# First-pass weight conversion: the low part's subtraction moved from VectorE to GpSimd

## The chip, the cores and the metric

The kernel runs on one core of a Trainium2 chip. The metric is the device time of one execution in microseconds; the kernel before takes 1091.99 us, the median of three runs (1090.27 to 1093.1).

## The reference

Linear attention over four batches, and two feed-forward blocks on its output:

```python
def phi(x):
    proj = np.einsum('bhsd,df->bhsf', x, w_phi)
    proj = proj - np.max(np.abs(proj), axis=-1, keepdims=True)
    return np.concatenate([np.exp(proj), np.exp(-proj)], axis=-1)
q_p, k_p = phi(q), phi(k)
kv = np.einsum('bhsf,bhsd->bhfd', k_p, v)
num = np.einsum('bhsf,bhfd->bhsd', q_p, kv)
den = np.einsum('bhsf,bhf->bhs', q_p, np.sum(k_p, axis=2))[..., None] + 1e-06
x = (num / den)              # 2304 tokens x 512 after a transpose
h = x @ w_in                 # 512 x 2048
x = np.maximum(0.01 * h, h) @ w_out          # 2048 x 512
g = x @ w_gate                               # 512 x 1536
out = (g / (1 + np.exp(-g)) * (x @ w_val)) @ w_out2   # 1536 x 512
```

The weights of the feed-forward blocks arrive as 64-bit floating point numbers.

## The kernel before, in words

The four batches of 576 tokens (b = 0 to 3) go through the kernel one after the other. The feed-forward blocks of batch b form one pass over all weights, and the attention of batch b + 1 is spread between the units of that pass. The attention of batch 0 stands alone at the start.

Every feed-forward product is split into three: a number is written as a high part that TensorE takes exactly (type float32r) and a low part, the rest. A product is then high x high, high x low and low x high. A unit (`u_l1`, `u_gate`, `u_val`, `u_out`, L645 to L694) makes one 128x576 result from 24 matmuls of 128x288.

There are 68 weight tiles of 128x512: 16 of kind "1" (w_in), 12 each of "g" and "v" (gate and value), 16 of "2" and 12 of "3" (the two output weights). In the first pass (b = 0) each of them goes through these steps:

- `w_load` (L493): SyncE's queue loads the 64-bit numbers into a `wi` buffer (five of them). `early` does the same for eight gate tiles during the attention of batch 0, with `gp` buffers.
- `w_to_f32` (L510): ScalarE (L519, L520, and L523 for kinds g, v and 3) and VectorE (L524, or L528 and L529, then L534) make a float32 tile in a `wr` buffer (four of them). Kinds 1, g and v are stored in DRAM as `kept`.
- `w_split` (L548) calls `to_wtile` (L543): ScalarE copies the float32 tile into the high part (L544), and a subtraction on VectorE makes the low part, float32 tile minus high part (L546, by the helper `sub`, which is recorded as L59). The result is a `wi` buffer for kinds 1, g and v and a `wo` buffer for kinds 2 and 3. The `wr` buffer is free after the subtraction.
- The `wo` tiles are stored in DRAM as `parts` by a DMA from GpSimd's queue (L565), for the later passes.

In the second pass (b = 1) the float32 tiles are read back and split again, and the split tiles are stored; later passes load most tiles already split. `to_wtile` is also called for the tiles of sums of weights (names ending in X and Y), in the second and later passes.

The order of the work: a list of the weights by the unit that needs them, each four units ahead (`slots`, L1007), drives `splits` (L1025), which keeps loads, conversions and splits a few weights ahead of one another. The program's planner then orders the instructions on each engine by its own model of their times. The order of the units on TensorE, of ScalarE's high parts and of some loads is pinned by tokens ("units", "weights", "loads").

GpSimd has little else: it fills the ones beside the attention's values (L122, into `pk` buffers) and issues the stores of L565. The fills wait until TensorE's matmul of L202 has released the buffer.

Of the kernel before, what the change touches and what calls it, by code (L numbers as in the profile page):

```python
# [7 lines left out]
F32 = mybir.dt.float32  # L8
# [5 lines left out]
ALU = mybir.AluOpType  # L14
# [27 lines left out]
def linear_attention_two_mlps(ctx: ExitStack, tc, qT, kT, vt, w_phi, w1, w2, wg, wv, w3, cst, out):  # L42
    nc = tc.nc
    act, dve, pe, pool = nc.scalar, nc.vector, nc.tensor, nc.gpsimd
# [9 lines left out]
    def T(shape, dt, tag, bufs, pool=sb):  # L54
        uid[0] += 1
        return pool.tile(shape, dt, tag=tag, name=f"{tag}_{uid[0]}", bufs=bufs)

    def sub(o, a, b):
        dve.tensor_tensor(out=o, in0=a, in1=b, op=ALU.subtract)  # L59
# [415 lines left out]
    def parts_tile(key):  # L475
        tag = ("wi", 5)
        if key[0] in "23":
            tag = ("vhl", 1) if key[1] == QB and key[2] % CH == CH - 1 else ("wo", 5)
        wtile[key] = t = T([P, 2, 512], F32R, *tag)
        return t  # L480
# [59 lines left out]
        kept[kind, f] = d = dram.tile([P, 512], F32, name=f"kept_{uid[0]}")  # L540
        nc.sync.dma_start(out=d, in_=t)

    def to_wtile(t, r):  # L543
        i = act.activation(t[:, 0], r, AF.Copy)  # L544
        tc.stamp_issue_order_token(i.ins, "weights")
        sub(t[:, 1], r, t[:, 0].bitcast(F32))  # L546

    def w_split(key):  # L548
        if key not in wf:
            return  # L550
        r = wf.pop(key)
        kind, b, f = key
        if len(kind) == 2:
            wtile[key] = pair = []
            for k in range(2):
                t = T([P, 2, 256], F32R, "kvh" if kind[1] == "X" else "kvl", 4)
                to_wtile(t, r[:, 256 * k : 256 * k + 256])
                pair.append(t)
            return
        t = parts_tile(key)  # L560
        to_wtile(t, r)
        if kind in "23":
            uid[0] += 1
            parts[kind, f] = d = dram.tile([P, 1024], F32, name=f"parts_{uid[0]}")
            pool.dma_start(out=d, in_=t.rearrange("p a n -> p (a n)").bitcast(F32))  # L565
        if b != 1:
            return
        unkept.append(((kind, f), t))
        if kind == "1":
            if f % 2 == 0:  # L570
                wf["even"] = r
                return
            even = wf.pop("even")
            mix(even, r)
            for name, x in (("1X", even), ("1Y", r)):
                t = T([P, 2, 512], F32R, "wi", 5)
                to_wtile(t, x)
                unkept.append(((name, f // 2), t))

    def mix(r0, r1):  # L580


        lo, hi = slice(0, 256), slice(256, 512)
        dve.tensor_tensor(out=r1[:, hi], in0=r1[:, lo], in1=r1[:, hi], op=ALU.add)
        sub(r1[:, lo], r0[:, lo], r1[:, lo])
        sub(r0[:, lo], r1[:, hi], r0[:, lo])
        sub(r0[:, hi], r0[:, hi], r0[:, lo])
# [437 lines left out]
    def splits(i):  # L1025
        for k in slots[i]:
            ahead(loaded, w_load, done[0] + 2)
            ahead(conv, w_to_f32, done[0] + 2)
            ahead(done, w_split, done[0] + 1)
            keep_all_but(2 if done[0] < len(order) and order[done[0]][1] < 2 else 0)  # L1030
            ahead(loaded, w_load, done[0] + depth())
# [119 lines left out]
```

## Time and profile before

| | |
|---|---|
| median of three runs | 1091.99 us |
| profiled execution | 1094.43 us, span 1092.6 us |
| mean granted TensorE clock | 0.997 |
| TensorE busy | 1062.8 us (97%) |
| VectorE busy | 808.8 us (74%) |
| ScalarE busy | 656.2 us (60%) |
| GpSimd busy | 21.8 us (2%) |

Times within the span are in microseconds from its start. The attention of batch 0 ends, and the first units begin, at about 67 us; the last tile of the first pass is split at about 351 us. In the rows PE is TensorE, PEld its weight loads, DVE VectorE, ACT ScalarE, POOL GpSimd, SP SyncE. The ends of matmuls are modelled, so overlapping matmuls can make TensorE look full while they are spaced out; their count in a stretch shows the spacing.

### The profile page before, as it was taken

The numbers are of one execution on the slowest core, as the hardware profiler recorded it, in microseconds if no ns is written. First come the engines' busy times: TensorE is split into PE (matmuls) and PEld (weight loads), VectorE is DVE, ScalarE is ACT, GpSimd is POOL, SyncE is SP. The second block draws the span as 40 slices with busy tenths as digits, with TensorE's granted clock in tenths as the row PEclk, the third lists the DMA queues.
The fourth block names the chain that finished last, engine by engine and source line by source line (L and its number), as shares of the span: only waits on it lengthen the run. The fifth ranks groups of instructions, "written<-read, shape, count | busy, mean of one in ns | idle before, by whom it ended". The sixth has DMA issues, their size and how long they took to land.

```text
span 1092.6 us, 20353 instructions
## 1 busy us (share of the span) xinstructions
PE 1062.8 (97%) x7560; PEld 1023.3 (94%) x7560; DVE 808.8 (74%) x1761; ACT 656.2 (60%) x1467; POOL 21.8 (2%) x56
## 2 busy tenths in 40 slices
PE   7889999999999999999999988999999999999998
PEld 6668999989899999999999988999999999999998
DVE  6897797888899888779676864857779742458473
ACT  7878886768777787546553575644542334426441
POOL 1000100000000000000000000000000000000000
PEclk9999999999999999999999998999999999999999
DMA  9736767555666887767454386346978768748652
GB/s 326 235 114 204 240 208 259 172 183 177 210 201 230 335 304 268 263 237 242 164 177 145 111 332 235 126 175 228 313 243 297 287 216 303 275 157 306 216 178 96
DMA packets 98771, 245.61 MB, mean 225 GB/s; under 512 B 19952, under 2 KB 28400, under 8 KB 98672
## 3 DMA queue, kind: packets, MB, share of 16 engines
q1 hardware_dynamic: 94640, 229.62, 60.6%
q0 software_dynamic: 4032, 14.68, 3.4%
q8 instruction: 60, 0.98, 0.4%
q14 instruction: 39, 0.32, 0.1%
HBM read 178.73 MB, written 65.54 MB: 224 GB/s over the span
## 4 chain that ended last, share of the span: by engine, by line
PE 80%; DMA 8%; ACT 6%; DVE 4%; issue 1%; SPq 1%; ACTq 0%; DVEq 0%
PE pm L615 55%; PE pa L741 8%; PE pm L741 4%; PE pa L202 4%; PE pa L393 3%; DMA wi<-in_w_dram 2%; DMA wi<-parts 2%; PE pa L161 2%; DMA wr<-kept 1%; ACT wr L519 1%; DMA sums<-wr 1%; DVE wr L534 1%; PE pm L301 1%; PE pa L346 1%; ACT wi L520 0%
## 5 line engine op out<-in xcount | busy, mean ns | idle before, releaser
L615 PE MATMUL pm<-xh,wi 128*128 128x288 f32 x1664 | 351.7, 298 | 2.4 <-DVE es L656 1.8
L615 PE MATMUL pm<-gp,wo 128*128 128x288 f32 x2256 | 337.5, 297 | 0.8 <-DVE acc L682 0.5
L615 PEld LDWEIGHTS pm<-gp,wo 128*128 128x128 f32 x2256 | 311.1, 188 | 5.2 <-issue 1.9
L615 PEld LDWEIGHTS pm<-xh,wi 128*128 128x128 f32 x1664 | 271.8, 188 | 6.8 <-DVE es L656 2.3
L615 PE MATMUL pm<-xl,wi 128*128 128x288 f32 x832 | 246.7, 297 | 0.0
L615 PEld LDWEIGHTS pm<-xl,wi 128*128 128x128 f32 x832 | 156.3, 188 | 1.4 <-issue 0.6
L682 DVE TENSOR_TENSOR acc<-pm,acc 128x288 f32<-128x288 f32 x160 | 70.5, 450 | 45.2 <-PE pm L615 43.1
L59 DVE TENSOR_TENSOR gp<-es,gp 128x576 fp32r<-128x576 f32 x94 | 70.5, 751 | 29.9 <-ACT gp L62 29.2
L62 ACT ACTIVATE gp<-es 128x576 fp32r<-128x576 f32 x94 | 64.3, 688 | 27.9 <-DVE es L663 22.8
L741 PE MATMUL pm<-xh,wi 128*128 128x288 f32 x304 | 71.6, 303 | 6.0 <-DMA wi<-parts 5.2
L59 DVE TENSOR_TENSOR wi<-wr,wi 128x512 fp32r<-128x512 f32 x96 | 64.8, 682 | 13.2 <-ACT wi L544 12.8
L544 ACT ACTIVATE wi<-wr 128x512 fp32r<-128x512 f32 x96 | 59.5, 633 | 13.1 <-PE pm L615 5.2
L741 PEld LDWEIGHTS pm<-xh,wi 128*128 128x128 f32 x304 | 53.2, 193 | 7.8 <-DVE fl L59 3.7
L59 DVE TENSOR_TENSOR fl<-ff,fh 128x512 fp32r<-128x512 f32 (+1 forms) x72 | 50.9, 712 | 11.0 <-ACT fh L62 10.8
L520 ACT ACTIVATE wi<-wi 128x512 int32<-128x512 uint32 x60 | 41.5, 692 | 23.1 <-DMA wi<-in_wv_dram 10.7
L519 ACT ACTIVATE wr<-wi 128x512 f32<-128x512 f32 x60 | 41.2, 690 | 16.4 <-DMA wi<-in_w_dram 8.6
L396 ACT ACTIVATE dn<-pa 64x288 f32<-64x288 f32 x64 | 26.0, 406 | 36.1 <-PE pa L393 35.2
L62 ACT ACTIVATE fh<-ff 128x512 fp32r<-128x512 f32 (+1 forms) x72 | 47.0, 664 | 0.8
L643 ACT ACTIVATE es<-pm 128x288 f32<-128x288 f32 x72 | 28.8, 418 | 29.7 <-PE pm L741 17.1
L741 PE MATMUL pm<-xl,wi 128*128 128x288 f32 x152 | 45.6, 300 | 0.0
L534 DVE TENSOR_TENSOR wr<-wr,wi 128x512 uint16<-128x512 uint16 x60 | 44.9, 751 | 0.8
L202 PE MATMUL pa<-ff,pk 128*128 128x256 f32 (+1 forms) x160 | 42.6, 383 | 2.4 <-issue 1.9
(192 smaller groups left out, 2073.4 us busy)
## 6 DMA issues: line engine op xcount, KB each, us to landing
wi<-parts SPq DMA_DIRECT2D x96, 512.0 KB, 5.9
wo<-parts SPq DMA_DIRECT2D x77, 512.0 KB, 6.6
parts<-wi SPq DMA_DIRECT2D x56, 512.0 KB, 4.6
wi<-in_w_dram SPq DMA_DIRECT2D x44, 512.0 KB, 5.1
wr<-kept SPq DMA_DIRECT2D x72, 256.0 KB, 4.2
parts<-wo POOLq DMA_DIRECT2D x28, 512.0 KB, 5.1
kept<-wr SPq DMA_DIRECT2D x40, 256.0 KB, 4.2
wi<-in_wv_dram SPq DMA_DIRECT2D x12, 512.0 KB, 4.1
```

The source lines that it names most:

```text
L59: dve.tensor_tensor(out=o, in0=a, in1=b, op=ALU.subtract)
L62: act.activation(o, a, AF.Copy)
L202: pe.matmul(ps[:, 256 * h : 256 * h + 256], v[:n, h].rearrange("p a d -> p (a d)"), part[b, j, s][:n, h].rearrange("p a f -> p (a f)"), st ...
L393: pe.matmul(ps, w, x, start=(i == 0), stop=(i == len(ops) - 1))
L519: act.activation(t, high.bitcast(F32), AF.Abs, scale=REBIAS)
L520: act.activation(low, low.bitcast(U32), AF.Copy, scale=2.0**-29)
L534: dve.tensor_tensor(out=t16, in0=t16, in1=e16, op=ALU.add)
L544: i = act.activation(t[:, 0], r, AF.Copy)
L615: m = pe.matmul(ps, w, x[:, c], start=(i == 0), stop=(i == n - 1))
L643: act.activation(o, i, AF.Prelu, alpha=0.01)
L682: dve.tensor_tensor(out=acc[o][:, t], in0=ps, in1=acc[o][:, t], op=ALU.add)
L741: m = pe.matmul(ps, a, b, start=start and n == 0, stop=stop and n == 5, skip_group_check=True)
```

## The change

`to_wtile` gets an argument for the engine that subtracts. For the 68 tiles of the first pass `w_split` passes GpSimd, for all others VectorE as before. The operation, its operands and their sizes stay. Other callers of `to_wtile` are not touched.

```diff
-    def to_wtile(t, r):
+    def to_wtile(t, r, eng=dve):
         i = act.activation(t[:, 0], r, AF.Copy)
         tc.stamp_issue_order_token(i.ins, "weights")
-        sub(t[:, 1], r, t[:, 0].bitcast(F32))
+        eng.tensor_tensor(out=t[:, 1], in0=r, in1=t[:, 0].bitcast(F32), op=ALU.subtract)
...
         t = parts_tile(key)
-        to_wtile(t, r)
+        to_wtile(t, r, dve if b else pool)
```

## Rows read from the trace of the kernel before

**Rows 1.** The page's first part: busy time, share, instructions of each engine.
```profile
PE 1062.8 (97%) x7560; PEld 1023.3 (94%) x7560; DVE 808.8 (74%) x1761; ACT 656.2 (60%) x1467; POOL 21.8 (2%) x56
```

**Rows 2.** Busy time by stretch, all engines; stretch, length, engines, clock, DMA.
```profile
core 0: us, PE busy (x) PEld busy (x) DVE busy (x) ACT busy (x) POOL busy (x), PEclk, DMA share, GB/s
67.00:100.00 33.00, 30.90 (x170) 26.69 (x169) 25.04 (x65) 24.74 (x69) 1.97 (x5) 1.00 0.42 130
...
175.00:205.00 30.00, 29.54 (x217) 28.36 (x216) 23.97 (x46) 19.55 (x39) 2.12 (x4) 1.00 0.63 207
205.00:285.00 80.00, 78.25 (x550) 74.16 (x549) 69.08 (x148) 61.06 (x126) 2.66 (x5) 1.00 0.51 163
285.00:310.00 25.00, 23.95 (x162) 21.71 (x161) 23.12 (x47) 22.77 (x47) 1.59 (x3) 1.00 0.78 262
310.00:352.00 42.00, 42.00 (x303) 40.57 (x302) 38.56 (x84) 31.45 (x67) 2.13 (x4) 1.00 0.58 193
...
205.00:352.00 147.00, 144.20 (x1010) 136.45 (x1009) 130.76 (x277) 115.29 (x238) 6.38 (x12) 1.00 0.58 188
```

**Rows 3.** Waits of TensorE, 67 to 352 us: total, times, longest.
```profile
PE pm L615 <- DVE es L656: 1.7, 1, 1.7
...
PE pm L615 <- DVE wi L59: 0.2, 1, 0.2
```

**Rows 4.** The chain of waits, 0 to 360 us: start, duration, link.
```profile
74.53 0.69 DVE wi L59
...
185.48 0.69 DVE wo L59
...
194.40 0.68 DVE wo L59
...
299.64 0.70 DVE wi L59
300.36 1.30 ACT wr L519 x2
```

**Rows 5.** Timeline of VectorE around 195 us: start, duration, instruction, wait before.
```profile
193.78 1.29 DVE L59 TENSOR_TENSOR wo<-wr,wo 128x512 fp32r<-128x512 f32 x2 [2.65 <-ACT wo L544]
...
195.23 0.43 DVE L528 TENSOR_SCALAR wr<-wr 128x512 int32<-128x512 int32 x1
```

**Rows 6.** Groups of VectorE by line, 0 to 352 us.
```profile
L59 DVE TENSOR_TENSOR wi<-wr,wi 128x512 fp32r<-128x512 f32 x42 | 28.7, 685 | 5.6 <-ACT wi L544 5.3
```

**Rows 7.** Waits of ScalarE, 67 to 352 us: total, times, longest.
```profile
ACT wr L519 <- DVE wi L59: 2.8, 6, 1.0
```

**Rows 8.** Groups of GpSimd by line, whole span.
```profile
L565 POOL DMA_DIRECT2D parts<-wo x28 | 15.2, 544 | 250.3 <-DVE wo L59 240.9 <-DVE top L348 8.8
L122 POOL MEMSET pk<- 128x256 f32 x16 | 4.9, 315 | 28.7 <-PE pa L202 26.5 <-issue 1.9 <-POOLq L1135 0.3
L122 POOL MEMSET pk<- 128x128 f32 x8 | 1.6, 204 | 50.7 <-issue 25.1 <-PE pa L202 16.9 <-DMA cst_sb<-in_cst_dram 8.7
```

**Rows 9.** Waits of GpSimd, whole span: total, times, longest.
```profile
POOL pk L122 <- PE pa L202: 43.4, 13, 7.9
```

**Rows 10.** Timeline of GpSimd around 139 us: start, duration, instruction, wait before.
```profile
139.30 0.20 POOL L122 MEMSET pk<- 128x128 f32 x1 [7.44 <-PE pa L202]
```

**Rows 11.** Groups of VectorE by line, 205 to 352 us.
```profile
L534 DVE TENSOR_TENSOR wr<-wr,wi 128x512 uint16<-128x512 uint16 x27 | 20.2, 753 | 0.0
L524 DVE SCALAR_TENSOR_TENSOR wr<-wr,wi 128x512 int32<-128x512 int32 x27 | 18.4, 681 | 7.3 <-ACT wi L523 7.3
L59 DVE TENSOR_TENSOR wi<-wr,wi 128x512 fp32r<-128x512 f32 x25 | 17.0, 683 | 0.8 <-ACT wi L544 0.7
...
L59 DVE TENSOR_TENSOR gp<-es,gp 128x576 fp32r<-128x576 f32 x13 | 9.7, 748 | 2.6 <-ACT gp L62 2.5
L59 DVE TENSOR_TENSOR wo<-wr,wo 128x512 fp32r<-128x512 f32 x12 | 8.2, 682 | 0.2 <-ACT wo L544 0.2
```

## The prediction

> **What bounds the kernel now.** I began with the busy shares: TensorE is busy for 97% of the span, VectorE 74%, ScalarE 60%, GpSimd 2% [rows 1]. The change touches only the first pass over the weights (b = 0), so I then cut that pass into stretches [rows 2]. The granted clock is 1.00 in all of them, so no term here belongs to the clock. VectorE is the fullest engine beside TensorE: 130.76 of 147 us between 205 and 352 us, which is 89%.
>
> A busy TensorE can still run thinly, because the ends of its matmuls are modelled, so I counted. Between 310 and 352 us it is busy throughout and runs 303 matmuls, 138.6 ns each. At that rate the 550 of 205 to 285 us need 76.2 us of 80, the 162 of 285 to 310 us need 22.5 us of 25, and the 217 of 175 to 205 us need all 30. The mix is richer in slower attention matmuls at 67 to 100 us, and there I take the plain gap, 33.0 - 30.9 = 2.1 us [rows 2]. So what a perfectly fed TensorE could win back in 67 to 352 us is 3.8 + 2.5 + 2.1 = 8.4 us, an estimate. This is the ceiling of the gain. The loss has no such ceiling.
>
> Who causes those gaps? TensorE waits for a converted weight's low part by name for only 0.2 us; its longest wait on VectorE is 1.7 us for an evicted gate [rows 3]. The chain of waits names the subtraction more often: six pieces after 67 us among its longest ones are this subtraction on VectorE, about 0.7 us each [rows 4] (the first, the last and two between stand there). At 193.78 us two subtractions run back to back for 1.29 us and the first step of the next weight's conversion (L528) starts behind them at 195.23 us [rows 5]: there the chain runs through VectorE's order, not through the data.
>
> **The change, part by part.** *Removed from VectorE:* 40 subtractions into wi and 28 into wo; the row of 0 to 352 us has 42 for wi, the last two of them from the second pass [rows 6]. 68 x 0.684 = 46.5 us leave VectorE. Nearly all of it lies beside TensorE's work, so it counts for the end only where the chain holds it. Of the six pieces, five are followed by other VectorE work that doesn't read their result. The first two of these stand side by side (wi, then wo at 75.6 us) and would follow one another on GpSimd's queue just so; I count one of the two. Without these four the chain is shorter by 4 x 0.68 = 2.7 us. The sixth, at 299.64 us, is followed by a ScalarE conversion step (L519) [rows 4], which fits a wait for a `wr` buffer: such waits are 2.8 us in six cases [rows 7]. There the subtraction itself is what counts, and it gets slower.
>
> *Added to GpSimd:* 68 subtractions of 128x512. The trace shows none on GpSimd. Its nearest rows are fills: 315 ns for 256 columns and 204 ns for 128 [rows 8], which is 0.867 ns a column and 93 ns fixed. A subtraction passes three streams (two read, one written). If all overlap it costs 93 + 444 = 0.54 us; if none does, 93 + 3 x 444 = 1.42 us. I take 1.2 us, nearer the upper end, since this engine's fills are already slow with one stream. The load is 68 x 1.2 = 82 us in a queue that holds 21.8 us of work now [rows 1], so GpSimd has room.
>
> The Trainium skill (GPSIMD Engine Reference, section 3.1) gives 4497 ns for a tensor_tensor of 2048 fp32 columns; a quarter, as an estimate, is 1.12 us, and the sum would be the same.
>
> *Latency:* a low part is ready 1.2 us after ScalarE's high part plus GpSimd's own queue, against 0.68 us plus VectorE's queue. The queue of an 89% busy engine costs about one instruction, so this comes out even to 0.6 us later. The cover is the plan: a weight is asked for four units ahead, and a unit of 24 matmuls lasts 24 x 138.6 ns = 3.3 us, so some 13 us. It is thin only where the conversion chain itself is late. The six `wr` waits grow by up to 0.74 us each (1.42 - 0.68), 4.4 us on ScalarE, of which I count 1.5 us on the path.
>
> *Order on GpSimd's queue:* behind a subtraction stand the store of the same tile (28 of 0.53 us, now on the engine that made the data) and the fills of the value tiles. Fills wait for TensorE to release a buffer, 43.4 us in 13 cases, the longest 7.9 us [rows 9]; a subtraction queued behind one waits too. The last fill of these is at 139.3 us [rows 10], and until there 13 us of lead cover 7.9 us, so I cost them at nothing; without the cover one is worth at most 7.9 us. SyncE's loads into `wr` begin only with the second pass; the last subtractions of the first release those buffers, late by the latency above. The planner reorders the queues by its model; no row prices that, and I let it move the result by one or two of the gaps above (2 to 4 us), either way.
>
> *VectorE held by GpSimd's reads:* whether two engines can read SBUF at the same time is not shown by any row here, since the fills read nothing. If they can't, hold per subtraction lies between 0 and 1.42 us. In 205 to 352 us, 23 + 12 = 35 subtractions move [rows 11, 2]: VectorE falls from 130.8 to 130.8 - 35 x 0.683 = 106.9 us. The forms that read two tiles from SBUF and stay (L534, L524, gp's low part: 20.2 + 18.4 + 9.7 = 48.3 us) are 45% of that [rows 11], with small forms left out. A hold of 0.45 to 0.6 x 1.2 us, so 0.54 to 0.72 us, would hand back 19 to 25 us of the 23.9 us.
>
> The Trainium skill (SBUF — State Buffer, section "Who interferes with whom") speaks against this change: a VectorE instruction with two SBUF inputs contends with a GpSimd instruction that reads SBUF, and the one that comes second is blocked for the whole of the first. By that rule VectorE is no freer than before; no run here shows it yet.
>
> Sum for the likeliest case: the profiled execution took 1094.43 us (span 1092.6). -2.7 + 1.5 = -1.2 us gives 1093.2 us. That execution is 2.4 us above the median of the runs, 1091.99 us, so against the median it is 1090.8, rounded to **1091 us**. Its own range is 1088.7 to 1095.3.
>
> **Rivals.**
> - *Faster, because VectorE is really freed.* Without a hold VectorE drops to 106.9 of 147 us, and the gaps at 205 to 310 us close: -6.3 us, 1085.7 us; with the gap at 67 to 100 us, 1083.6 us. For it: in the chain the next conversion steps stand behind subtractions [rows 5]. Against it: VectorE also waits for ScalarE in this stretch (7.3 us for L523 alone [rows 11]), and ScalarE keeps all its work.
> - *Slower, because the pair takes turns.* If GpSimd's reading holds VectorE for the whole subtraction, 205 to 352 us decides: VectorE's room is 147 - 106.9 = 40.1 us over 35 subtractions, so the turn comes at 1.15 us of hold each. At 1.42 us the stretch needs 106.9 + 49.7 = 156.6 us, 9.6 us more than it has: 1101.6 us. At 1.2 us it is full, and any late eviction stops TensorE; then I expect +5 us, 1097 us. For it: conversions come in bursts, so the next weight's two-input steps want to run just then. Against it: VectorE spends half its time in forms that read one SBUF tile or PSUM.
> - *The change moves the work, but nothing changes,* since TensorE never waits for it: 1092 us. It lies inside the forecast's range and speaks for it: 0.2 us of named waits [rows 3].
>
> **How the numbers follow.** About 0.3%, 3.3 us, is what a measurement of this kernel can tell from no change. Forecast (with the rival that nothing changes): 0.40. Freed VectorE: 0.28, all of it faster by over 0.3%. Held VectorE: 0.32, slower by over 0.3%; the `wr` waits growing on the path are counted in it. The range goes from 1084.5, near the closed gaps, to 1101.5, the full hold at the upper price.
>
> **What would show it.** Right: 68 subtractions on GpSimd of 1.1 to 1.4 us; VectorE's busy time of 205 to 352 us within 8 us of before although 35 instructions are gone, its two-input forms longer on average (L534 above 0.75 us); TensorE's matmul count of that stretch as before. The freed case would show L534 and L524 unchanged at 0.75 and 0.68 us and over 560 matmuls in 205 to 285 us. The held case would show VectorE above 140 us of 147 there and TensorE waiting for evictions by VectorE or ScalarE. Wrong in the working itself: a subtraction on GpSimd above 1.42 us, waits for `wo` or `wi` low parts named on TensorE, or a difference that arises after 352 us.

## The result, and the profile after

The changed kernel takes 1104.76 us (median of six runs, 1099.19 to 1106.67) where the kernel before took 1092.09 us beside it: the ratio is 1.0108, with an interval of 1.0091 to 1.0126. It is slower by 1.1%, outside the stated range and on the side to which the prediction gave 0.32. Of the runs below, one execution, the profiled one of the fills beside the kernel before (1116.81 us), was in a slower state; its time is left out, and only lengths and places are read from its profile.

The page's first part of the changed kernel, answering [rows 1]:

```profile
PE 1066.3 (97%) x7560; PEld 1025.0 (93%) x7560; DVE 795.9 (72%) x1693; ACT 655.0 (59%) x1467; POOL 115.3 (10%) x124
```

The work moved as planned: 68 instructions fewer on VectorE, 68 more on GpSimd. But VectorE is only 12.9 us freer, not 46.5 us. The instructions that stayed on it are longer by 26 us in all. The rest of the 33.6 us is overlap: neighbouring instructions overlap in the trace (before the change VectorE's lengths add up to 905 us where it is busy for 808.8 us), so an instruction that goes frees less than its length.

Busy time by stretch of the changed kernel (columns as in [rows 2]):

```profile
67.00:100.00 33.00, 30.87 (x167) 26.50 (x167) 22.80 (x59) 24.55 (x67) 7.15 (x7) 1.00 0.43 135
100.00:205.00 105.00, 99.76 (x669) 95.25 (x668) 74.42 (x131) 76.20 (x180) 41.16 (x44) 0.97 0.66 223
205.00:352.00 147.00, 142.65 (x989) 133.78 (x988) 121.86 (x238) 114.04 (x232) 54.08 (x46) 1.00 0.57 191
```

The middle stretch in the kernel before, in the same view:

```profile
100.00:205.00 105.00, 104.54 (x728) 100.74 (x728) 85.98 (x171) 84.41 (x197) 8.75 (x19) 1.00 0.73 246
```

The count of matmuls tells where the time went. Between 100 and 205 us TensorE runs 669 instead of 728; at the 138.6 ns that the prediction took for one, 59 of them are 8.2 us. Between 205 and 352 us 989 instead of 1010 are 2.9 us [rows 2]. The sum, 11.1 us, is the whole difference of the spans (1102.4 - 1092.6 = 9.8 us) and a little more; the changed kernel was four matmuls ahead at 100 us. And VectorE is *less* busy in both stretches: it fell from 85.98 to 74.42 us and from 130.76 to 121.86 us [rows 2]. TensorE lost its time while VectorE had more room than before.

GpSimd's groups in the changed kernel (line, operation, count, busy us, mean ns, idle before):

```profile
L546 POOL TENSOR_TENSOR wi<-wr,wi 128x512 fp32r<-128x512 f32 x40 | 54.9, 1375 | 181.8 <-ACT wi L544 173.1 <-DMA kept<-wr 4.2 <-DMA pk<-in_vt_dram 2.2
L546 POOL TENSOR_TENSOR wo<-wr,wo 128x512 fp32r<-128x512 f32 x28 | 39.0, 1407 | 13.9 <-ACT wo L544 13.9
```

VectorE's groups of the changed kernel, 0 to 365 us:

```profile
L534 DVE TENSOR_TENSOR wr<-wr,wi 128x512 uint16<-128x512 uint16 x60 | 51.0, 851 | 1.2
L59 DVE TENSOR_TENSOR gp<-es,gp 128x576 fp32r<-128x576 f32 x29 | 25.9, 895 | 8.1 <-ACT gp L62 8.0
L529 DVE SCALAR_TENSOR_TENSOR wr<-wi,wr 128x512 int32<-128x512 int32 x32 | 24.9, 777 | 0.5
L524 DVE SCALAR_TENSOR_TENSOR wr<-wr,wi 128x512 int32<-128x512 int32 x28 | 22.3, 796 | 11.6 <-issue 6.9 <-ACT wi L523 4.6
L528 DVE TENSOR_SCALAR wr<-wr 128x512 int32<-128x512 int32 x32 | 16.3, 509 | 24.5 <-ACT wr L519 24.5
L411 DVE TENSOR_TENSOR xf<-pa,rb 64x288 f32<-64x288 f32 x32 | 14.3, 448 | 0.8
L663 DVE SCALAR_TENSOR_TENSOR es<-pm,es 128x288 f32<-128x288 f32 x24 | 10.6, 445 | 0.1
```

The same groups in the kernel before, in the same stretch (L524 took 681 ns there too [rows 11]):

```profile
L534 DVE TENSOR_TENSOR wr<-wr,wi 128x512 uint16<-128x512 uint16 x60 | 44.9, 751 | 0.8
...
L529 DVE SCALAR_TENSOR_TENSOR wr<-wi,wr 128x512 int32<-128x512 int32 x32 | 21.8, 684 | 0.6
L59 DVE TENSOR_TENSOR gp<-es,gp 128x576 fp32r<-128x576 f32 x29 | 21.7, 750 | 4.5 <-ACT gp L62 4.4
...
L411 DVE TENSOR_TENSOR xf<-pa,rb 64x288 f32<-64x288 f32 x32 | 14.3, 446 | 0.6
...
L528 DVE TENSOR_SCALAR wr<-wr 128x512 int32<-128x512 int32 x32 | 13.4, 423 | 11.4 <-ACT wr L519 11.4
L663 DVE SCALAR_TENSOR_TENSOR es<-pm,es 128x288 f32<-128x288 f32 x24 | 10.6, 445 | 0.2 <-PE pm L615 0.2
```

The forms with two inputs in SBUF grew on average: L534 from 751 to 851 ns, L529 from 684 to 777, gp's low part from 750 to 895, L524 from 681 to 796. So did the one-input L528, from 423 to 509 ns. The forms with one input in PSUM (L411, L663) kept their length to 2 ns. The Trainium skill (SBUF — State Buffer, section "Who interferes with whom") draws just this line: a VectorE instruction with two SBUF inputs contends with a GpSimd instruction that reads SBUF, one in a two-port mode with any GpSimd instruction, and one that has a single SBUF input and no such mode with none. The trace agrees on every form shown here, though it doesn't show which mode L528 runs in.

How a stretched conversion step stops TensorE is to be seen in the timeline of the changed kernel around its second stop (start, duration, engine, instruction, idle time before it and what ended it):

```profile
167.25 2.77 POOL L546 TENSOR_TENSOR wo<-wr,wo 128x512 fp32r<-128x512 f32 x2
167.58 1.30 DVE L528 TENSOR_SCALAR wr<-wr 128x512 int32<-128x512 int32 x1 [1.63 <-ACT wr L519]
...
168.91 1.67 DVE L529 SCALAR_TENSOR_TENSOR wr<-wi,wr 128x512 int32<-128x512 int32 x1
...
170.61 0.75 DVE L534 TENSOR_TENSOR wr<-wr,wi 128x512 uint16<-128x512 uint16 x1
...
171.43 0.33 SPq L505 DMA_DIRECT2D wi<-in_w_dram  x1
...
177.48 0.66 ACT L519 ACTIVATE wr<-wi 128x512 f32<-128x512 f32 x1 [3.38 <-DMA wi<-in_w_dram]
...
178.61 0.69 ACT L643 ACTIVATE es<-pm 128x288 f32<-128x288 f32 x2
```

and TensorE's first matmul behind them:

```profile
179.05 0.61 PE L615 MATMUL pm<-xh,wi 128*128 128x288 f32 x1 [2.58 <-ACT es L643]
```

Two subtractions run on GpSimd from 167.25 us for 2.77 us. VectorE's L528 and L529 start beside them and take 1.30 and 1.67 us instead of 0.42 and 0.68, so they end 1.87 us late. L534 behind them is the last reader of a `wi` buffer; only when it ends does SyncE issue the load of the next weight, at 171.43 us. ScalarE's next instruction is L519 of that weight, so ScalarE stands still for 3.38 us, and the eviction L643 stands behind it. TensorE waits 2.58 us for that eviction. If everything behind L529 had come 1.87 us earlier, some 0.7 us of that wait would be left, an estimate. In all, SyncE's loads of weights wait longer for L534 than before (0 to 360 us; before, then after):

```profile
SPq L505 <- DVE wr L534: 67.7, 20, 11.2
```

```profile
SPq L505 <- DVE wr L534: 84.3, 20, 9.6
```

The two longest groups of TensorE's waits, 67 to 352 us, in the changed kernel (total, times, longest):

```profile
PE pm L615 <- ACT es L643: 2.8, 2, 2.6
PE pm L615 <- ACT gp L62: 2.1, 1, 2.1
```

They are waits for ScalarE, whose own work the change leaves alone (0.2 and 0.3 us before). The other groups, up to 1.8 us each, name ScalarE and VectorE; none names GpSimd. The stops cost more than they last, as the stretches of 10 us with them show:

```profile
140.00:150.00 10.00, 7.89 (x44) 7.30 (x44) 6.03 (x12) 8.51 (x22) 2.71 (x3) 0.83 0.93 318
...
170.00:180.00 10.00, 7.42 (x47) 6.91 (x46) 4.24 (x8) 4.69 (x11) 1.60 (x4) 0.94 0.89 324
180.00:190.00 10.00, 10.00 (x67) 9.84 (x67) 7.37 (x13) 8.66 (x20) 2.60 (x2) 0.88 0.81 261
```

After each stop the granted clock falls, to 0.83, 0.94 and 0.88 on average, that is to the lower of its levels (1.2 instead of 2.4 GHz) for part of the stretch (the last two belong to the same stop). Over 100 to 205 us it is 0.97 instead of 1.00: some 3 of the 8.2 us, an estimate (0.03 x 105 us).

### The profile page after: what moved, and what is told of

Its sections match the earlier page's. It is cut to its first block, busy times and chain, and to the rows that moved or that the text cites. A ratio compares the mean times of both kernels' runs of the same rounds, so it can differ in the third digit from the quotient of the medians.

```text
span 1102.4 us, 20385 instructions
## 1 busy us (share of the span) xinstructions
PE 1066.3 (97%) x7560; PEld 1025.0 (93%) x7560; DVE 795.9 (72%) x1693; ACT 655.0 (59%) x1467; POOL 115.3 (10%) x124
## 4 chain that ended last, share of the span: by engine, by line
PE 64%; DMA 11%; ACT 8%; DVE 7%; issue 6%; POOL 2%; SPq 1%; POOLq 0%; DVEq 0%; ACTq 0%
PE pm L615 43%; PE pa L741 8%; DMA wi<-in_w_dram 5%; PE pm L741 4%; PE pa L202 2%; PE pa L393 2%; DMA wi<-parts 2%; DMA wi<-in_wv_dram 2%; POOL wi L546 1%; DVE wr L534 1%; DMA wr<-kept 1%; ACT wr L519 1%; PE pa L161 1%; DVE wr L529 1%; ACT wi L520 1%
## 5 line engine op out<-in xcount | busy, mean ns | idle before, releaser
L59 DVE TENSOR_TENSOR gp<-es,gp 128x576 fp32r<-128x576 f32 x94 | 74.7, 796 | 35.5 <-ACT gp L62 34.8
L546 POOL TENSOR_TENSOR wi<-wr,wi 128x512 fp32r<-128x512 f32 x40 | 54.9, 1375 | 181.8 <-ACT wi L544 173.1
L519 ACT ACTIVATE wr<-wi 128x512 f32<-128x512 f32 x60 | 41.0, 684 | 27.0 <-DMA wi<-in_w_dram 11.7
L534 DVE TENSOR_TENSOR wr<-wr,wi 128x512 uint16<-128x512 uint16 x60 | 51.0, 851 | 1.2
L643 ACT ACTIVATE es<-pm 128x288 f32<-128x288 f32 x72 | 29.9, 430 | 26.7 <-PE pm L741 16.0
```

The costliest lines, as they stand in the source:

```text
L519: act.activation(t, high.bitcast(F32), AF.Abs, scale=REBIAS)
L534: dve.tensor_tensor(out=t16, in0=t16, in1=e16, op=ALU.add)
L546: eng.tensor_tensor(out=t[:, 1], in0=r, in1=t[:, 0].bitcast(F32), op=ALU.subtract)
L643: act.activation(o, i, AF.Prelu, alpha=0.01)
```

## The experiments

Three theories were put against each other. **Hold:** GpSimd's reads of SBUF block VectorE's two-input and two-port forms; conversions, loads, ScalarE and TensorE follow as above. **Late low part:** the subtraction takes twice as long on GpSimd, whatever VectorE does. **Order:** the planner orders all engines anew (on ScalarE some 380 places differ between the orders of the two traces), and the new order happens to be worse. All ratios are to runs of the kernel before on the same chip (its medians there were 1093.1 to 1093.8 us).

**Fills in place of subtractions.** The low parts of the first pass are left out. The first fill also covers the high part's last column, so that it waits for the high part as the subtraction did.

```diff
-        eng.tensor_tensor(out=t[:, 1], in0=r, in1=t[:, 0].bitcast(F32), op=ALU.subtract)
+        flat = t.rearrange("p a n -> p (a n)").bitcast(F32)
+        # on GpSimd: three fills, from the high part's last column on
+        for n in (513, 513, 128): pool.memset(flat[:, 511:511 + n], 0.0)
```

> In place of each of the 68 subtractions GpSimd fills the low part with zeros by three fills of 513, 513 and 128 columns (about 1.3 us together, from the fills' 0.867 ns a column and 93 ns), which wait for the high part and read nothing; the low parts of the first pass are left out of the products. Theory hold (GpSimd's reads of SBUF block VectorE's two-input and two-port forms, the conversions come late, the loads behind them come late, ScalarE stands on a load and TensorE on ScalarE): the loss of 12.7 us is gone, 1084 to 1094 us, L534 back at 0.75 us and L529 at 0.68 us on average. Theory late low part (1.3 us on GpSimd instead of 0.68 us on VectorE, whatever VectorE does): 1099 to 1106 us. Theory order (the planner's other order alone): 1099 to 1106 us, since the work on each engine is planned as in the changed kernel.

Measured: 1098.56 us, ratio 1.0038 (1.0019 to 1.0058). Two thirds of the loss are gone with the reads. VectorE's groups in this kernel:

```profile
L534 DVE TENSOR_TENSOR wr<-wr,wi 128x512 uint16<-128x512 uint16 x60 | 45.3, 755 | 1.0
...
L529 DVE SCALAR_TENSOR_TENSOR wr<-wi,wr 128x512 int32<-128x512 int32 x32 | 22.0, 687 | 0.6
...
L528 DVE TENSOR_SCALAR wr<-wr 128x512 int32<-128x512 int32 x32 | 19.2, 600 | 26.9 <-ACT wr L519 26.7
```

L534 and L529 are back at their old lengths. The one-input L528 is even longer, 600 ns on average, so a writing GpSimd still blocks that one. The median L528 takes 427 ns as before; a few take up to 2.4 us. The longest starts while GpSimd makes fills without a gap and ends only behind the last of them:

```profile
163.53 2.69 POOL L546 MEMSET wo<- 128x513 f32 x7
164.08 2.42 DVE L528 TENSOR_SCALAR wr<-wr 128x512 int32<-128x512 int32 x1 [1.46 <-ACT wr L519]
```

Hold had predicted at most 1094 us and the others at least 1099. The time lies between, just below the others' bound, while the two-input forms did what hold had said. So the reads account for about two thirds of the loss, and 0.4% is left for blocked L528, lateness and order together.

**A shadow subtraction beside the kernel before.** VectorE does all its old work; GpSimd reads the same tiles for nothing.

```diff
         sub(t[:, 1], r, t[:, 0].bitcast(F32))
+        if shadow:      # b == 0
+            pool.tensor_tensor(out=scratch, in0=t[:, 0], in1=t[:, 0], op=ALU.subtract)
```

> The kernel before, VectorE subtracts as before; beside each first-pass tile GpSimd subtracts the high part from itself into a scratch tile that nobody reads: 68 reads of SBUF on GpSimd, and nothing waits for them but their buffers. Theory hold: VectorE is blocked and not relieved, at least as slow as the changed kernel, 1102 to 1125 us, VectorE's L534 above 0.82 us on average. Theory late low part: 1089 to 1095 us, for every low part is made by VectorE. Theory order: within 4 us of 1092 us.

Measured: 1112.86 us, ratio 1.0169 (1.0149 to 1.019), as hold said and against the other two: no wait in the trace names these results. L534 grew less than hold said (786 ns, not over 820), because here the subtractions take the blow, as they start together with their shadows. VectorE keeps its subtractions here and becomes nearly full: it is busy for 141.33 of the 147 us from 205 to 352 us, where TensorE runs 934 matmuls instead of 1010. So this run shows that the reads cost time. It does not tell a full VectorE from single late steps.

**The same with fills.**

> As the shadow subtraction beside the kernel before, but GpSimd only fills the same scratch tile three times (512, 512, 128 columns, about 1.3 us): it writes SBUF and reads nothing. Theory hold: 1089 to 1095 us, VectorE's forms at their old lengths. Theory late low part: 1089 to 1095 us. Theory order: this one has its own order, so any time within 4 us of the shadow subtraction's is what it predicts.

Measured: 1101.51 us, ratio 1.0062 (1.0044 to 1.008). All three theories missed: hold and late low part had said 1095 us at most, order within 4 us of 1112.86 us. It is not the control it was meant to be. The fills wait for nothing but their buffers, so GpSimd makes nearly all of them at the start, where it is busy for 66.15 of the first 67 us, and the last 15 from 94 to 99 us. L534 and L529 kept their lengths. L528 is at 596 ns on average because one of them took 5.21 us beside those last 15 fills; its median is 427 ns. A cast of 128x10, 0.16 us in the kernel before, started beside 87 fills in a row and ended with the last of them:

```profile
44.15 31.00 POOL L547 MEMSET shadow<- 128x512 f32 x87
```

```profile
59.13 16.05 DVE L316 CAST mm<-mq 128x10 fp32r<-128x10 f32 x1
```

So where GpSimd's instructions follow one another without a gap, the block of a one-input form can last as long as the row, not only as long as one instruction.

**More buffers for the float32 tiles.** The changed kernel, kinds 2 and 3 converted into four more buffers.

```diff
-        t = T([P, 512], F32, "wr", 4)
+        t = T([P, 512], F32, *(("kvl", 4) if key[0] in "23" else ("wr", 4)))
```

> The changed kernel with four more buffers for the float32 tiles: those of kinds 2 and 3 go into kvl buffers, which are idle in the first pass. Theory late low part, in the form that the float32 buffers are held longer by GpSimd and ScalarE waits for them (6.3 us of named waits in the changed kernel): at most 1099 us. Theory hold: 1101 to 1108 us, the waits for buffers shrink but VectorE's stretched forms stay.

Measured: 1120.64 us, ratio 1.0234 (1.0209 to 1.0258): both theories missed. The experiment did not remove what it was meant to remove: ScalarE waits 7.7 us for GpSimd's subtractions between 67 and 352 us, against 6.3 us in the change. So it says nothing on what the held `wr` buffers cost, and why it got slower still stays open.

**The shadow with 32 and with 256 columns.** The cleanest test: the same 68 instructions at the same places of the program, only the length of the read differs. (The planner's order on ScalarE still differs between these three traces, by some 200 to 330 places.)

> The shadow subtraction beside the kernel before, cut from 512 to 32 columns: the same 68 instructions at the same places, each reading SBUF for a sixteenth. Theory hold: the loss of the full shadow (1.7%) nearly goes, 1090 to 1098 us, VectorE's subtractions back at 0.68 to 0.72 us from 0.91 (wi) and 1.13 us (wo). Theory order: the 68 instructions upset the planner as before, 1104 to 1116 us.

> The shadow subtraction beside the kernel before with 256 columns: between 32 columns (ratio 1.0004) and 512 (1.0169). Theory hold, with a blocked time that grows with the columns read: GpSimd's instruction near 0.95 us, VectorE's subtractions into wo between 0.72 and 1.1 us, 1096 to 1106 us. Theory order: no dependence on the columns.

Measured: 1094.26 us, ratio 1.0004 (0.9987 to 1.0021) with 32 columns, and 1097.37 us, 1.0044 (1.0027 to 1.0062) with 256, against 1.0169 with 512. The loss grows with the columns that GpSimd reads, and with 32 columns none is measured. Order predicted no dependence. VectorE's subtraction into wo at 32, 256 and 512 columns:

```profile
L59 DVE TENSOR_TENSOR wo<-wr,wo 128x512 fp32r<-128x512 f32 x28 | 19.2, 700 | 0.2
```

```profile
L59 DVE TENSOR_TENSOR wo<-wr,wo 128x512 fp32r<-128x512 f32 x28 | 24.1, 872 | 0.2 <-ACT wo L544 0.2
```

```profile
L59 DVE TENSOR_TENSOR wo<-wr,wo 128x512 fp32r<-128x512 f32 x26 | 29.1, 1133 | 0.0
```

700, 872 and 1133 ns, from 682 in the kernel before [rows 11].

**An order alone.** Both kernels with one number of the plan nudged, which in the kernel before moves on ScalarE some 560 places of the trace, more than the change does.

```diff
-                with tc.high_priority(offset=50):
+                with tc.high_priority(offset=60):
```

> The kernel before with one number of the plan nudged (the attention's priority offset 60 in place of 50): the same instructions on the same engines, another order on every engine, on ScalarE about as many places as the change moves. Theory hold: within 5 us of 1092 us, an order alone costs less than the change. Theory order: an order of that distance costs 5 us or more.

> The changed kernel with the same nudge: to be compared with the nudged kernel before, not with 1092 us. Theory hold: 8 to 20 us slower than the nudged kernel before. Theory order: the pair differs by chance, within 4 us.

Measured: the kernel before nudged 1091.98 us, ratio 0.999 (0.9973 to 1.0008); the changed kernel nudged 1108.72 us, 1.013 (1.0106 to 1.0154), 16.7 us apart. The change loses as much and more in another order, and that order alone loses nothing. So order is not the cause of the whole.

**Pieces.** The changed kernel, each subtraction in four of 128 columns: the low part comes later, a single read is shorter.

```diff
-            eng.tensor_tensor(out=t[:, 1], in0=r, ...)
+            for c in four slices of 128 columns:
+                eng.tensor_tensor(out=t[:, 1, c], in0=r[:, c], ...)
```

> The changed kernel with each first-pass subtraction on GpSimd in four pieces of 128 columns: GpSimd needs some 4 x 0.72 = 2.9 us for a tile in place of 1.39 us (0.55 us for 32 columns and 1.75 ns for each further column, from the shadows), so a low part is twice as late, while a single read holds VectorE for a quarter. Theory hold: no slower than the changed kernel, 1094 to 1106 us, and VectorE's longest conversion steps below 1.2 us from 1.7 us. Theory late low part: 1110 us or more.

Measured: 1100.06 us, ratio 1.0062 (1.0045 to 1.0079): faster than the change in one piece, although GpSimd works longer. Its groups there:

```profile
L548 POOL TENSOR_TENSOR wi<-wr,wi 128x128 fp32r<-128x128 f32 x160 | 83.5, 552 | 140.1 <-ACT wi L544 136.5 <-DMA pk<-in_vt_dram 3.6
L548 POOL TENSOR_TENSOR wo<-wr,wo 128x128 fp32r<-128x128 f32 x112 | 64.9, 612 | 8.1 <-ACT wo L544 8.1
```

A tile takes 4 x 0.552 = 2.2 us and more instead of 1.38 us. (The expectation's 0.72 us a piece came from 0.55 us for 32 columns, an average over instructions that VectorE held up; the shortest of these took 0.23 us.) L534 and L529 in the view of their source lines (minimum, median, maximum in ns), first in the change, then in pieces:

```profile
L534 DVE TENSOR_TENSOR wr<-wr,wi x60: 701/758/1737, 13.3 to 358.0; 128x512 uint16<-128x512 uint16 x60
...
L529 DVE SCALAR_TENSOR_TENSOR wr<-wi,wr x32: 651/693/1676, 12.0 to 204.5; 128x512 int32<-128x512 int32 x32
```

```profile
L534 DVE TENSOR_TENSOR wr<-wr,wi x60: 696/760/1030, 13.3 to 356.8; 128x512 uint16<-128x512 uint16 x60
...
L529 DVE SCALAR_TENSOR_TENSOR wr<-wi,wr x32: 651/693/2218, 12.1 to 194.0; 128x512 int32<-128x512 int32 x32
```

The median instruction is not blocked at all. The longest L534 falls from 1737 to 1030 ns, below the 1.2 us that hold had named. L529 goes against that sign: its longest grows from 1676 to 2218 ns. It starts at 108.74 us beside four pieces that follow one another without a gap until 110.40 us, and ends at 110.96 us. So pieces in a row can block a step for as long as one long read.

The stretches of this kernel (columns as in [rows 2]), and ScalarE's waits for GpSimd, 67 to 352 us:

```profile
100.00:205.00 105.00, 101.51 (x712) 98.20 (x710) 76.65 (x140) 81.29 (x188) 68.09 (x125) 1.00 0.70 242
205.00:352.00 147.00, 140.50 (x956) 131.08 (x957) 114.01 (x232) 110.69 (x226) 75.68 (x142) 0.99 0.55 177
```

```profile
ACT wr L519 <- POOL wo L548: 8.9, 5, 2.5
ACT wr L519 <- POOL wi L548: 8.4, 10, 1.5
```

The gain lies between 100 and 205 us, 712 matmuls instead of the change's 669. Between 205 and 352 us TensorE runs 956, fewer than the change's 989, and ScalarE waits 17.3 us for GpSimd instead of 6.3 us. Late low part, which said 1110 us or more, falls as the whole cause. A low part that comes later may still cost something of its own; no run separates that from the hold.

**Parts of the change.** Only wo, only wi, only kinds g, v and 3 on GpSimd: `pool if b == 0 and kind in "23"`, `"1gv"`, `"gv3"` in place of `dve if b else pool`.

> Only the 28 subtractions into wo go to GpSimd, the 40 into wi stay on VectorE. Theory hold: 28 of 68 holds and 28 of 68 of the relief, some 5 us slower than before, 1094 to 1102 us. Theory order: any time between 1088 and 1106 us.

> Only the 40 subtractions into wi go to GpSimd, the 28 into wo stay on VectorE. With wo alone the ratio was 1.0016 and with both 1.0108. Theory hold, added up by tile: some 10 us slower than before, 1099 to 1107 us. If the losses of the two don't add up because it takes both to fill VectorE in the same moments: 1093 to 1098 us.

> Only kinds g, v and 3 on GpSimd: the 36 tiles that are converted from about 200 us on. The changed kernel lost 60 of 85 matmuls before 205 us and 25 behind. Theory hold, by that count: 25 x 139 ns = 3.5 us slower than before, 1094 to 1100 us. Theory order: any time between 1088 and 1106 us.

Measured: wo alone 1095.75 us, ratio 1.0016 (1.0001 to 1.0031); wi alone 1105.68 us, 1.0109 (1.0089 to 1.013); the late kinds 1099.1 us, 1.0055 (1.0036 to 1.0074). The late kinds cost 6.0 us where the count of matmuls had said 3.5 us, inside the range of the expectation. The surprise is the split by buffer: 28 of 68 subtractions cost 0.16%, and the other 40 alone cost as much as the whole change.

**The hold alone, by kind.** The 512-column shadow beside wi or wo only.

> The shadow subtraction (512 columns, VectorE subtracts as in the kernel before) beside the 40 wi tiles alone. If the hold itself falls in worse moments for wi: most of the full shadow's 1.69%, ratio 1.011 to 1.017 (1105 to 1112 us). If wi costs more in the change because its low part is wanted sooner: 40 of 68 of it, ratio about 1.010 or less, and wo's shadow takes the rest.

> The same beside the 28 wo tiles alone. If the hold falls in better moments for wo: ratio 1.000 to 1.004 (1092 to 1098 us). If a hold costs the same at either: 28 of 68 of 1.69%, ratio about 1.007 (1101 us).

Measured: 1101.36 us, ratio 1.0083 (1.0062 to 1.0104) beside wi, and 1101.2 us, 1.0079 (1.0056 to 1.0102) beside wo; the two add up to the full shadow's 1.7%. So the 28 holds beside wo cost as much as the 40 beside wi, and the moments are not better for wo. Of the two readings on record, worse moments for wi missed (1.011 at least). The other, a low part of wi that is wanted sooner, kept inside its range, but no run shows that lateness itself. Moving wo gives most of it back (0.79% as a shadow, 0.16% when VectorE's own subtraction goes), moving wi gives nothing back (0.83% and 1.09%). Why moving the subtraction helps with wo and not with wi is not settled. ScalarE's waits for a float32 buffer don't tell the two apart: with wo alone it waits 5.4 us for VectorE's wi subtractions, with wi alone 6.0 us for GpSimd's.

No version that moves work to GpSimd beat the kernel before.

## Why the prediction was wrong

Nothing contradicts the view of the bound: 8.4 us of gaps on TensorE in the first pass, so little to win and no ceiling to the loss. The cost of a subtraction on GpSimd held: 1.38 us on average (1.30 us in the median), inside the bounds of 0.54 to 1.42 us and above the 1.2 us taken.

The estimate from the figure of the Trainium skill (GPSIMD Engine Reference, section 3.1), 1.12 us, is below every one of the 68, of which the shortest took 1.26 us. A quarter of a long instruction leaves out most of the fixed part: the shortest rows of 128 and of 512 columns, 0.444 and 1.263 us, give 2.13 ns a column and 0.17 us fixed, an estimate.

The step that failed is the pricing of the hold, in size and in kind. In size: the hand-back was forecast as 19 to 25 us of 23.9 us between 205 and 352 us. VectorE fell by 8.9 us there, from 130.76 to 121.86 us. But with the fills, where L534 and L524 keep their lengths, it fell only to 114.11 us, that is by 16.7 us and not by 23.9 us, because the lengths overlap. So the hold handed back some 8 us (121.86 - 114.11, an estimate from two kernels). In kind: the prediction weighed the hold only as a share of VectorE's busy time. It concluded that VectorE is "no freer than before", and its sum has no term for the hold, which priced it at nothing for the end. In its place the runs showed that GpSimd's shadow reads of 512 columns cost 1.69% (some 18 us) when no work is moved, while those of 32 columns cost nothing, and that without the reads two thirds of the change's 12.7 us are gone. In the change VectorE is less busy than before, and yet single steps of its conversions (L524, L528, L529, L534) last up to 1.8 us instead of 0.4 to 0.8 us; the stop at 176 to 179 us shows how such a step delays a load, and behind the load ScalarE and TensorE. That each lost microsecond goes this way is argued from that stop, not shown.

The rival "slower, because the pair takes turns" had the right mechanism in the wrong place. It let the loss begin only where VectorE is full, from 1.15 us of hold each in 205 to 352 us, and gave 5 to 9.6 us there. That stretch lost 2.9 us. The rest was lost at 100 to 205 us, where VectorE stands at 71% (82% before) and the rival saw nothing. Of that stretch the prediction had counted only 175 to 205 us, and found no gap on TensorE there.

The sum's first term, -2.7 us from four subtractions that leave the chain, is not to be seen: in each of the stretches 67 to 100, 100 to 205 and 205 to 352 us the changed kernel runs fewer matmuls. The second, +1.5 us for `wr` waits, rests on waits that were near in size (ScalarE waits 6.3 us for GpSimd's subtractions instead of 3.0 us for VectorE's); no run shows whether they lie on the path. The loads into `wr` don't begin with the second pass, as the prediction had it: SyncE issues them from 176.52 us on in the kernel before. Up to 360 us SyncE stands 34.3 us for these buffers behind GpSimd's subtractions, against 33.2 us behind VectorE's before, so this path did not grow. That fills on GpSimd's queue cost nothing held as far as the waits show: no wait on TensorE names them between 67 and 352 us. The reordering, let in for 2 to 4 us, measured nothing in the one other order of the kernel before (0.999).

Of the signs named beforehand, those of the held case came true in part: L534 was longer (851 ns) and TensorE waited for evictions by ScalarE, but VectorE was far from 140 us of 147. Of the forecast's own signs, GpSimd's subtractions and the longer L534 came true; VectorE's busy time fell by more than 8 us, and the count of matmuls did not stay.

## What to carry to other kernels

Before elementwise work goes to GpSimd, look which of VectorE's forms read two SBUF tiles or run a one-input form from SBUF to SBUF, and whether one of them frees a buffer that a load waits for. There a blocked step can stop whoever stands behind the load, however idle VectorE is on average. An average load says whether an engine can take work, not what a block costs. If work must go there, short pieces cost less here than long ones (0.62% against 1.08%), though they keep GpSimd busy longer. Pieces that follow one another without a gap can still block like one long instruction.

## What the runs showed of the hardware

The block grows with the columns read: VectorE's subtraction into wo averages 700, 872 and 1133 ns beside shadows of 32, 256 and 512 columns. With 32 columns VectorE's groups of conversions and subtractions keep their length to 18 ns.

The block goes both ways. GpSimd's shadow of 32 columns takes 0.23 us at its shortest; where it starts beside a subtraction on VectorE it takes about 0.68 us, as long as that subtraction (21 of the 68). The averages of GpSimd's instructions contain such blocks. Their shortest are 0.23, 0.60 and 1.03 us at 32, 256 and 512 columns when one tile is read twice (0.17 us and 1.67 ns a column, an estimate), and 0.44 and 1.26 us at 128 and 512 columns when two tiles are read.

A GpSimd that only fills leaves the two-input L534 and L529 alone (755 and 687 ns), while it stretches the one-input L528 from 423 to 600 ns on average. And a row of GpSimd's instructions without a gap can block as a whole: L528 for 2.42 us beside seven fills, L529 for 2.22 us beside four pieces of a subtraction, a cast for 16.05 us beside the end of 87 fills.
